# Conversion of the feed-forward weights spread over more steps of an attention and feed-forward kernel

## The chip, the cores and the metric

The kernel runs on one core of a Trainium2 chip. The metric is the device time of one execution in microseconds (us). PE is the matrix engine (TensorE), DVE is VectorE, ACT is ScalarE, POOL is GpSimd and SP is the engine that issues the DMAs (SyncE).

## The reference

Talking-heads attention over 4 batches, 12 heads, 448 positions and 64 columns a head is followed by a gated feed-forward over 1792 tokens of width 768, with a hidden width of 2048.

```python
scores = scale * np.matmul(q, k.transpose(0, 1, 3, 2))
scores = np.einsum('bhij,hg->bgij', scores, w_pre)
scores = scores - np.max(scores, axis=-1, keepdims=True)
attn = np.exp(scores)
attn = attn / (np.sum(attn, axis=-1, keepdims=True) + 1e-09)
attn = np.einsum('bhij,hg->bgij', attn, w_post)
attn_out = np.matmul(attn, v)
...
h = x @ w_in
g = h * (1.0 / (1.0 + np.exp(-1.702 * h)))
return (g @ w_out).astype(np.float32)
```

The two feed-forward weights arrive as 64-bit floats, everything else as 32-bit floats.

## The kernel before

**Steps.** The attention is cut into steps of ten query positions with all twelve heads, 120 rows a step (`GI` times `H`). A batch has 45 steps (`GPB`), the kernel 180 (`N`), and the main loop counts them in `i`. A step multiplies its gathered scores `r` by the mixing matrix on PE (`mix`, L279), takes the row maximum on DVE (`peak`, L286), the exponential on ACT (`expo`, L293), a sum correction on POOL (L299) and the reciprocal on DVE (`inverse`, L304); then it weighs the mixing matrix or the rows on POOL (L309, or L329 and L343 from the second batch on), multiplies again on PE (`post_whole` L319 in the first batch, `post` L356 to L358 after it) and copies the result (`keep_whole` L375; `keep_upper` L379 and `keep_lower` L383). Since L286 runs once a step, its rows mark the steps in the trace: the first, at 34.75 us, is step 0. The scores themselves (`scores`, L233 in 32-bit floats for batches 0 and 1, L243 in pairs of 16-bit floats for the others) are computed ahead, sent to DRAM (`sd`, L258) and gathered from there four steps ahead (`gather`, L269). `context` (L397, L408) multiplies by v. Batch 0's context is complete around step 57, so from step 58 on the loop has feed-forward work of a finished batch beside the attention of the next one.

**Feed-forward.** A unit is one slice of 256 hidden columns (`NS` = 8 slices) for one batch: 32 units, in batch order. Its work is cut into twelve quanta: six parts of the first product (`h`, L588, gate on ACT L606 and DVE L609 and L616) and six of the second (`po`, L627, collected on DVE L657 or on ACT and POOL). The loop owes 2.15 quanta a step (`RATE`) from step 58 on. What remains after step 180 runs with nothing beside it.

**Conversion of the weights.** Each slice of each kind (w_in is kind 0, w_out kind 1) has to be turned from 64-bit floats into a pair of 16-bit floats once: 16 conversions, numbered n = 2s + kind. `convert` splits one into three parts of 128x512. For each part it loads the words (L477), runs five integer or float operations on DVE (L484, L488, L492, L498, L504, tile `w_f`) and a sum of squares on ACT (L96). When the three sums are there, a small matmul joins them (L108), DVE reads the sum (L109) and derives the scale in six small operations; then ACT writes the three upper halves (`w_upper`, L532), DVE the three lower ones (`w_lower`, L537, from `w_f` too), and SP stores the pair to DRAM (L543, tile `wd`). `fetch_w` (L576) loads a slice from there for each unit (tile `wt`), one unit ahead.

**What sets the order.** Engines run their queues in order, and the order is made when the kernel is built. Conversions are jobs. In each step `run_jobs(i)` emits, after `peak` and `expo` of the step and before its `inverse`, all jobs whose first step has come, whose predecessors ran, and whose engine has tokens left (a budget of 4.3 us a step, 5.2 once feed-forward runs, at most 4.5 saved). `begin`, the argument `first` of `convert`, is the step at which the loads of a conversion may start; its two-step lag puts the DVE work two steps later. Only in those places does it act: a slice that is converted later is also fetched later, since `fetch_ahead` waits for its store.

Of the kernel before, what the change touches and what calls it, by code (L numbers as in the profile page):

```python
# [28 lines left out]
NPAIR = H // 2  # L29
NR, CP = 4, S // 4  # L30
NCC = DM // 128
NS = 8
# [6 lines left out]
def attention_then_feed_forward(ctx, tc, q, k, v, w_pre, w_post, w_in, w_out, out):  # L39
# [422 lines left out]
    EARLY = -20  # L462
# [297 lines left out]
    conv_done = {}  # L760
    for s in range(NS):
        for kind in range(2):
            n = s * 2 + kind
            conv_done[kind, s] = convert(kind, s, n * 5 - NPAIR if n > 1 else EARLY + 10 * n)


    quanta = []
# [303 lines left out]
```

## Time and profile before

| | |
|---|---|
| runs of the kernel before | 1024.65, 1029.36, 1032.99 us, median 1029.36 us |
| profiled execution | 1027.42 us, its span 1025.7 us |
| mean granted PE clock in it | 0.961 of full speed |
| busy in the span | PE 90%, DVE 61%, ACT 59%, POOL 35% |

The span lies between the first and the last instruction that the profile holds; the 1.7 us beside it are start and end. Busy shares over the span mix three stages: the first batch without feed-forward work (to 257.92 us, the start of step 58), attention and feed-forward side by side (to step 180), and feed-forward alone.

### The profile page before, as it was taken

The numbers are of one execution on the slowest core, as the hardware profiler recorded it, in microseconds if no ns is written. First come the engines' busy times: TensorE is split into PE (matmuls) and PEld (weight loads), VectorE is DVE, ScalarE is ACT, GpSimd is POOL, SyncE is SP. The second block draws the span as 40 slices with busy tenths as digits, with TensorE's granted clock in tenths as the row PEclk, the third lists the DMA queues.
The fourth block names the chain that finished last, engine by engine and source line by source line (L and its number), as shares of the span: only waits on it lengthen the run. The fifth ranks groups of instructions, "written<-read, shape, count | busy, mean of one in ns | idle before, by whom it ended". The sixth has DMA issues, their size and how long they took to land.

```text
span 1025.7 us, 19868 instructions
## 1 busy us (share of the span) xinstructions
PE 925.0 (90%) x7344; PEld 542.4 (53%) x7344; DVE 628.8 (61%) x1389; ACT 605.2 (59%) x1380; POOL 354.5 (35%) x536
## 2 busy tenths in 40 slices
PE   5678878877899889999899999999899999999998
PEld 4345555544455444555455555656455666555554
DVE  5658786698976796554644575555645565443334
ACT  3666768677577676765657657656656564323332
POOL 0111111145433455343533454334534444001221
PEclk9888999888999998999999999999999999999999
DMA  8988979768557656654676647546654341234322
GB/s 301 289 275 313 332 267 323 259 197 245 190 198 244 232 187 181 192 172 131 202 225 207 202 150 234 166 130 179 212 164 146 108 148 64 93 123 151 118 93 85
DMA packets 66565, 198.19 MB, mean 193 GB/s; under 512 B 7668, under 2 KB 32372, under 8 KB 66468
## 3 DMA queue, kind: packets, MB, share of 16 engines
q1 hardware_dynamic: 66064, 196.83, 59.4%
q8 instruction: 58, 0.95, 0.4%
q14 instruction: 39, 0.32, 0.1%
q10 hardware_dynamic: 404, 0.09, 0.1%
HBM read 140.27 MB, written 56.62 MB: 192 GB/s over the span
## 4 chain that ended last, share of the span: by engine, by line
PE 62%; DVE 17%; ACT 8%; DMA 8%; issue 3%; POOL 1%; SPq 0%; ACTq 0%; DVEq 0%; POOLq 0%
PE po L627 19%; PE h L588 18%; PE mx L279 8%; PE av L408 4%; PE qk L243 3%; PE pp L356 2%; PE pp L358 2%; PE pp L357 2%; DVE w_p L537 2%; DMA sd<-sc 2%; ACT waste L96 2%; DVE w_f L504 2%; DMA w<-in_moe_w_out_dram 2%; DVE nm L286 2%; ACT e L293 1%
## 5 line engine op out<-in xcount | busy, mean ns | idle before, releaser
L627 PE MATMUL po<-g,wt 128*128 128x448 f16 x1152 | 243.8, 355 | 11.3 <-DVE th L609 6.8
L588 PE MATMUL h<-x,wt 128*128 128x448 f16 x1152 | 244.1, 356 | 3.9 <-ACT sc L253 2.9
L279 PE MATMUL mx<-r,wa 120*120 120x448 f32 x360 | 183.3, 592 | 40.0 <-ACT e L293 29.7
L343 POOL TENSOR_TENSOR a<-w,a 120x448 f16<-120x448 f32 x135 | 150.8, 1117 | 130.2 <-issue 71.5
L627 PEld LDWEIGHTS <-wt 128*128 128x128 f16 x1152 | 109.4, 99 | 130.0 <-issue 45.1
L588 PEld LDWEIGHTS <-wt 128*128 128x128 f16 x1152 | 109.2, 98 | 117.0 <-issue 31.2
L329 POOL TENSOR_SCALAR w<-e,rs 120x448 f32<-120x448 f32 x135 | 88.2, 653 | 227.3 <-DVE rs L304 217.8
L337 ACT ACTIVATE a<-e,rs 120x448 f16<-120x448 f32 x135 | 91.0, 674 | 106.1 <-DVE rs L304 106.1
L657 DVE SCALAR_TENSOR_TENSOR acc<-po,ct,acc 128x448 f32<-128x448 f32 x141 | 96.1, 682 | 74.3 <-PE po L627 72.2
L293 ACT ACTIVATE e<-mx,nm 120x448 f32<-120x448 f32 x180 | 113.6, 631 | 31.2 <-POOL wr L309 25.4
L609 DVE SCALAR_TENSOR_TENSOR th<-th,h 128x448 f32<-128x448 f32 x64 | 39.7, 620 | 137.8 <-ACT th L606 137.8
L606 ACT ACTIVATE th<-h,ct 128x448 f32<-128x448 f32 x64 | 40.5, 633 | 140.2 <-PE h L588 129.6
L253 ACT COPY sc<-qk 120x448 f32<-120x448 f32 (+1 forms) x186 | 89.6, 532 | 41.8 <-PE qk L233 28.9
L286 DVE TENSOR_REDUCE nm<-mx 120x1 f32<-120x448 f32 x180 | 108.9, 605 | 1.9 <-PE mx L279 1.9
L356 PE MATMUL pp<-wp,a 120*112 120x120 f16 x540 | 95.7, 220 | 14.8 <-DVE p L383 14.3
L279 PEld LDWEIGHTS mx<-r,wa 120*120 120x120 f32 x360 | 61.6, 193 | 83.9 <-ACT e L293 47.0
L299 POOL TENSOR_SCALAR rs<-sm 120x1 f32<-120x1 f32 x180 | 56.8, 315 | 115.8 <-ACT e L293 103.8
L358 PE MATMUL pp<-wp,a 120*112 120x120 f16 x540 | 95.1, 219 | 0.0
L357 PE MATMUL pp<-wp,a 120*112 120x120 f16 x540 | 94.9, 218 | 0.0
L383 DVE TENSOR_TENSOR p<-pp,p 112x480 f16<-112x480 f32 x135 | 87.2, 647 | 5.9 <-ACT p L379 5.9
L356 PEld LDWEIGHTS <-a 120*112 120x112 f16 x540 | 71.5, 132 | 26.9 <-DVE p L383 12.1
L357 PEld LDWEIGHTS <-a 120*112 120x112 f16 x540 | 71.8, 133 | 15.9 <-issue 9.5
(126 smaller groups left out, 1258.1 us busy)
## 6 DMA issues: line engine op xcount, KB each, us to landing
wt<-wd SPq DMA_DIRECT2D x64, 768.0 KB
r<-sd SPq DMA_DIRECT2D x176, 210.0 KB
sd<-sc SPq DMA_DIRECT2D x72, 420.0 KB
w<-in_moe_w_in_dram SPq DMA_DIRECT2D x24, 512.0 KB
w<-in_moe_w_out_dram SPq DMA_DIRECT2D x24, 512.0 KB
wd<-w_p SPq DMA_DIRECT2D x16, 768.0 KB
sd<-sc SPq DMA_DIRECT2D x24, 308.0 KB
out_dram<-acc SPq DMA_DIRECT2D x24, 224.0 KB
```

Source lines behind the costliest of these rows:

```text
L253: (nc.scalar.copy if engs[x] == "A" else nc.vector.tensor_copy)(t[:n, x, :], two[x][:n, :S])
L279: nc.tensor.matmul(mx[:K, :S], st["wa", b][:K, :K], row.pop(("r", i))[:K, :], start=True, stop=True)
L286: nc.vector.tensor_reduce(nm[:K], row["mx", i][:K, :S], axis=AX.X, op=ALU.max, negate=True)
L293: nc.scalar.activation(e[:K], row.pop(("mx", i))[:K, :S], AF.Exp, bias=row.pop(("nm", i))[:K, 0:1], scale=1.0, accum_out=sm[:K, 0:1],)
L337: nc.scalar.activation(a1[:K], row.pop(("e", i))[:K], AF.Copy, scale=row.pop(("rs", i))[:K, 0:1])
L343: nc.gpsimd.tensor_tensor(a2[:K], row.pop(("w", i))[:K], row["a1", i][:K], op=ALU.subtract)
L356: nc.tensor.matmul(o, a1[:K, js], wp1[:K, :, :n], start=True, stop=False)
L357: nc.tensor.matmul(o, a1[:K, js], wp2[:K, :, :n], start=False, stop=False)
L358: nc.tensor.matmul(o, a2[:K, js], wp1[:K, :, :n], start=False, stop=True)
L588: nc.tensor.matmul(h, w[:, i, c, fc * 128:(fc + 1) * 128], x[:, j, c, :], start=(n == 0), stop=(n == len(terms) - 1),)
L627: nc.tensor.matmul(po, w[:, j, fc, e * 128:(e + 1) * 128], g[:, i, fc, :], start=(n == 0), stop=(n == len(terms) - 1),)
L657: nc.vector.scalar_tensor_tensor(a, po, c, a, op0=ALU.mult, op1=ALU.add)
```

## The change

One line gives each conversion its first step. Conversions 0 and 1 keep theirs. Before, conversion n began at step 5n - 6: at 4, 9, 14 and so on to 69. Now it begins at 7n - 12 up to n = 8 (2, 9, 16, 23, 30, 37, 44), and then every five and a half steps (49, 55, 60, 66, 71, 77, 82). Steps 49 on hold the loads of conversion 11 before and of conversion 9 now. Sizes, operations, and the order of the feed-forward quanta stay as they were.

```diff
     for s in range(NS):
         for kind in range(2):
             n = s * 2 + kind
-            conv_done[kind, s] = convert(kind, s, n * 5 - NPAIR if n > 1 else EARLY + 10 * n)
+            begin = EARLY + 10 * n if n < 2 else 7 * n - 12 if n <= NS else 11 * (n - NS) // 2 + 7 * NS - 12
+            conv_done[kind, s] = convert(kind, s, begin)
```

Counting the six conversion instructions on DVE (L484 to L504 and L537) by step in the two built programs gives: steps 9 to 43, 126 before and 90 now; steps 44 to 57, 46 and 44; steps 58 to 77, 57 and 59; steps 78 to 94, 8 and 44; none later. A whole conversion has 18 of them.

DVE in step 17, from one row maximum to the next, before: `w_1_p` is the pair of slice 1, `w_2_f` the words of slice 2.

```order
L286 TENSOR_REDUCE nm_921<-mx_867 120x1
L537 SCALAR_TENSOR_TENSOR w_1_p<-w_1_f_713,w_1_s,w_1_p 128x512
L537 SCALAR_TENSOR_TENSOR w_1_p<-w_1_f_719,w_1_s,w_1_p 128x512
L537 SCALAR_TENSOR_TENSOR w_1_p<-w_1_f_781,w_1_s,w_1_p 128x512
L498 SCALAR_TENSOR_TENSOR w_2_f_894<-w_2_64_1_821,w_2_f_894 128x512
L504 SCALAR_TENSOR_TENSOR w_2_f_894<-w_2_64_1_821,w_2_f_894 128x512
L304 RECIPROCAL rs_926<-rs_926 120x1
L286 TENSOR_REDUCE nm_963<-mx_911 120x1
```

The same step now.

```order
L286 TENSOR_REDUCE nm_911<-mx_860 120x1
L537 SCALAR_TENSOR_TENSOR w_1_p<-w_1_f_717,w_1_s,w_1_p 128x512
L537 SCALAR_TENSOR_TENSOR w_1_p<-w_1_f_723,w_1_s,w_1_p 128x512
L537 SCALAR_TENSOR_TENSOR w_1_p<-w_1_f_760,w_1_s,w_1_p 128x512
L304 RECIPROCAL rs_916<-rs_916 120x1
L286 TENSOR_REDUCE nm_949<-mx_901 120x1
```

The lower halves of one slice no longer share a step with the words of the next slice: the two conversions overlapped before, and now one follows the other.

DVE in step 83, before: `ct` is a unit's scale, `th` the gate, `acc` the collected output, `p` the lower half of the attention rows.

```order
L286 TENSOR_REDUCE nm_4748<-mx_4668 120x1
L600 TENSOR_SCALAR ct_4791<-ex,ew 128x1
L609 SCALAR_TENSOR_TENSOR th_0_4793<-th_0_4793,h_0_4726 128x448
L637 TENSOR_TENSOR ct_4359<-eo,ew 128x1
L657 SCALAR_TENSOR_TENSOR acc_2974<-po_0_4799,ct_4359,acc_2974 128x448
L383 TENSOR_TENSOR p_2_3900<-pp_4702,p_2_3900 112x48x10
L304 RECIPROCAL rs_4753<-rs_4753 120x1
```

The same step now.

```order
L286 TENSOR_REDUCE nm_4681<-mx_4591 120x1
L484 TENSOR_SCALAR w_7_f_4689<-w_7_64_2_4304 128x512
L488 TENSOR_SCALAR w_7_f_4689<-w_7_f_4689 128x512
L492 TENSOR_SCALAR w_7_f_4689<-w_7_f_4689 128x512
L498 SCALAR_TENSOR_TENSOR w_7_f_4689<-w_7_64_2_4304,w_7_f_4689 128x512
L504 SCALAR_TENSOR_TENSOR w_7_f_4689<-w_7_64_2_4304,w_7_f_4689 128x512
L600 TENSOR_SCALAR ct_4732<-ex,ew 128x1
L609 SCALAR_TENSOR_TENSOR th_0_4734<-th_0_4734,h_0_4659 128x448
L637 TENSOR_TENSOR ct_4267<-eo,ew 128x1
L383 TENSOR_TENSOR p_2_3801<-pp_4635,p_2_3801 112x48x10
L304 RECIPROCAL rs_4686<-rs_4686 120x1
```

Five instructions of the last w_in slice now stand ahead of the gate, of `p`'s lower half and of the reciprocal; one collection of `acc` went to ACT and POOL.

SP around the fetch of that slice for unit 7, before: `wt_7` is that slice; its store `wd_7_113` lies 21 rows above the fetch.

```order
L269 DMA r_4974<-sd_0_98 120x448
L576 DMA wt_7_4976<-wd_7_113 128x3072
L258 DMA sd_1_99<-sc_1_0_4969 120x896
L269 DMA r_5049<-sd_0_98 120x448
L269 DMA r_5137<-sd_0_98 120x448
L576 DMA wt_6_5139<-wd_6_120 128x3072
```

The same place now.

```order
L576 DMA wt_6_5111<-wd_6_120 128x3072
L258 DMA sd_1_99<-sc_1_1_5094 120x896
L269 DMA r_5202<-sd_0_98 120x448
L543 DMA wd_7_113<-w_7_p 128x3072
L269 DMA r_5295<-sd_0_98 120x448
L576 DMA wt_7_5297<-wd_7_113 128x3072
```

The store now stands one gather ahead of the fetch that reads what it wrote (steps 89 and 90; the fetch stood in step 86 before). PE's first product of unit 7 stands in step 93 in both.

## Rows read from the trace of the kernel before

**Rows 1.** The page: busy times of the engines, and two of them in 40 slices.

```profile
PE 925.0 (90%) x7344; PEld 542.4 (53%) x7344; DVE 628.8 (61%) x1389; ACT 605.2 (59%) x1380; POOL 354.5 (35%) x536
...
PE   5678878877899889999899999999899999999998
...
DVE  5658786698976796554644575555645565443334
```

**Rows 2.** Windows between steps: busy PE, PEld, DVE, ACT, POOL (instructions), PEclk, DMA share, GB/s.

```profile
63.93:192.84 128.91, 104.82 (x682) 67.11 (x681) 99.35 (x254) 92.93 (x236) 23.42 (x70) 0.92 0.88 298
...
257.92:497.81 239.89, 217.94 (x1883) 125.86 (x1883) 165.55 (x351) 163.45 (x373) 105.77 (x143) 0.96 0.62 197
389.95:463.62 73.67, 72.13 (x606) 41.94 (x604) 40.52 (x96) 48.41 (x110) 30.84 (x47) 0.98 0.64 197
497.81:721.62 223.81, 214.20 (x1936) 126.65 (x1935) 126.98 (x275) 143.49 (x330) 98.34 (x140) 0.99 0.61 187
...
300.70:384.73 84.03, 72.65 (x608) 41.37 (x606) 66.71 (x140) 59.22 (x136) 37.62 (x47) 0.98 0.70 233
538.23:609.50 71.27, 67.09 (x610) 39.80 (x608) 39.84 (x93) 49.76 (x116) 31.63 (x45) 1.00 0.61 191
```

**Rows 3.** Windows, instructions on `w_f` on DVE alone: DVE busy (instructions), PEclk, DMA, GB/s.

```profile
63.93:192.84 128.91, 68.81 (x126) 0.92 0.88 298
...
257.92:497.81 239.89, 46.58 (x65) 0.96 0.62 197
300.70:384.73 84.03, 27.38 (x37) 0.98 0.70 233
389.95:463.62 73.67, 2.94 (x3) 0.98 0.64 197
```

**Rows 4.** DVE's timeline: starts of steps 10, 12, 16 to 21, 88 and 93, one L537.

```profile
65.74 0.60 DVE L286 TENSOR_REDUCE nm<-mx 120x1 f32<-120x448 f32 x1
...
79.17 0.60 DVE L286 TENSOR_REDUCE nm<-mx 120x1 f32<-120x448 f32 x1
...
91.25 0.60 DVE L286 TENSOR_REDUCE nm<-mx 120x1 f32<-120x448 f32 x1
...
95.81 0.61 DVE L286 TENSOR_REDUCE nm<-mx 120x1 f32<-120x448 f32 x1
...
96.33 2.07 DVE L537 SCALAR_TENSOR_TENSOR w_p<-w_f,w_s,w_p 128x512 f16<-128x512 f32 x3
...
99.72 0.61 DVE L286 TENSOR_REDUCE nm<-mx 120x1 f32<-120x448 f32 x1
...
103.03 0.60 DVE L286 TENSOR_REDUCE nm<-mx 120x1 f32<-120x448 f32 x1
...
104.84 0.61 DVE L286 TENSOR_REDUCE nm<-mx 120x1 f32<-120x448 f32 x1
...
108.25 0.61 DVE L286 TENSOR_REDUCE nm<-mx 120x1 f32<-120x448 f32 x1
...
434.49 0.61 DVE L286 TENSOR_REDUCE nm<-mx 120x1 f32<-120x448 f32 x1
...
458.07 0.60 DVE L286 TENSOR_REDUCE nm<-mx 120x1 f32<-120x448 f32 x1
```

**Rows 5.** One window of eight steps, columns as in rows 2.

```profile
88.03:111.67 23.64, 22.31 (x186) 15.15 (x186) 18.95 (x51) 18.46 (x46) 4.58 (x15) 1.00 0.92 319
```

**Rows 6.** Waits from 63.93 to 192.84 us: total, times, longest.

```profile
DVE w_n L109 <- PE pp L108: 14.0, 7, 4.7
```

**Rows 7.** The page's groups by line: POOL's costliest, and the row maximum.

```profile
L343 POOL TENSOR_TENSOR a<-w,a 120x448 f16<-120x448 f32 x135 | 150.8, 1117 | 130.2 <-issue 71.5
...
L286 DVE TENSOR_REDUCE nm<-mx 120x1 f32<-120x448 f32 x180 | 108.9, 605 | 1.9 <-PE mx L279 1.9
```

**Rows 8.** SP's timeline: the fetch of `wt_7`.

```profile
422.93 0.35 SPq L576 DMA_DIRECT2D wt<-wd  x1
```

**Rows 9.** The chain that ended last, from 30 to 430 us: its longest store.

```profile
49.80 9.79 DMA wd<-w_p
```

## The prediction

> **What bounds the kernel now.** I read the page first, then windows cut at the starts of steps, then DVE's timeline inside them. The page shows PE busy 90% of the span, but its slices show PE at 5 to 8 tenths and DVE at 5 to 9 in the first ten, and the reverse from the twentieth on [rows 1]. So a mean says little here: the change takes work out of one stage and puts it into another, and each has its own limit.
>
> L286 runs once a step, 180 times [rows 7], so step numbers can be turned into times. Two stretches matter, because the count of instructions in the order says so: 36 conversion instructions on DVE, two conversions of 18, leave steps 9 to 43 and come back in steps 78 to 94. Elsewhere the counts change by two instructions, up in one stretch and down in another.
>
> Steps 9 to 43 take 128.91 us; PE is busy 104.82 of it, DVE 99.35, ACT 92.93, and the DMA engines have a share of 0.88 [rows 2]. No engine is full; they take turns. A step without conversion work lasts 1.81 us (from 63.93, where that window begins, to 65.74), while the five steps from 91.25 to 108.25 last 4.56, 3.91, 3.31, 1.81 and 3.41, together 17.00, with one conversion among them [rows 4]. In the long ones DVE is the last to end: the reciprocal and the next row maximum stand behind the words of a slice in its queue, and exponential, POOL and the next matmul wait for them. But PE has no room either: in the eight steps from 88.03 to 111.67 it is busy 22.31 of 23.64 us [rows 5].
>
> In steps 80 to 94 PE is busy 72.13 of 73.67 us, DVE only 40.52 [rows 2]. PE is the bound there, and three conversion instructions are left in it [rows 3].
>
> **The change, first stretch.** Price of what leaves: 68.81 us over 126 instructions is 546 ns each [rows 3], so 36 of them are 19.7 us of DVE time. Two joins go with them, at which DVE waited for PE's small matmul 14.0 us in seven times, 2.0 each [rows 6]. The six sums and six upper halves on ACT, the six loads and two stores on SP's queue go too; with a DMA share of 0.88 that cannot hurt here.
>
> How much of it is on the path has two bounds. Upper: step lengths alone. The new cycle has seven steps: eight words of a slice in one (4.56 as step 16), six instructions in the next (6 x 0.546 and a row maximum of 0.60, 3.88), one instruction that fits into the gap (1.81), an empty step (1.81), the join (3.41), the upper halves on ACT (1.81), and the three lower halves (2.07 and 0.60, 2.67) [rows 4, 7]; the sum is 19.95. Five such cycles in place of seven of 17.00 give 99.8 for 119.0: a gain of 19.2 us. Lower: PE's idle time alone. It is 128.91 - 104.82 = 24.1 us. Steps 10 and 11 take 13.43 together [rows 4], 7.4 more than PE's mean of 2.99 a step; the first loads are late there, and the change does not thin them out. The other 16.7 us over 126 instructions are 0.132 each, 4.8 us for 36. I take **9 us**, nearer to the lower end, because the light steps that the change makes cannot last 1.81 us where a step carries scores and context: PE's own mean is 2.99, and the window of eight steps shows it almost full [rows 2, 5].
>
> **The change, second stretch.** The same 36 instructions cost more here: 46.58 us over 65 is 717 ns each against 546 [rows 3], so 25.8 us of DVE. What runs beside them differs: in steps 9 to 43 POOL is busy 18% of the time, in steps 80 to 94 it is 42% [rows 2]. The Trainium skill (SBUF — State Buffer, Who interferes with whom) says that DVE and POOL share a pair of ports as an exclusive lock, and that the second to come is blocked until the first is done; an estimate by it, half of POOL's 1117 ns operation [rows 7] in 42% of the cases, would make 546 into 781 ns, and the 25.8 us into 28.1. The trace agrees in direction and gives the smaller number, so the sum stays with the row.
>
> How much of 25.8 us is on the path: lower bound nothing, since DVE idles 73.67 - 40.52 = 33.2 us in steps 80 to 94 [rows 2]; upper bound all of it. Between them two comparisons of like with like. Steps 58 to 102 and 103 to 147 are two batches with the same attention and feed-forward work; the first has 65 conversion instructions more and takes 239.89 instead of 223.81 us [rows 2, 3]: 16.1 / 65 = 0.247 each. Steps 65 to 78 and 110 to 123, where the next batch's q and k are also converted, take 84.03 and 71.27 with 37 instructions more [rows 2, 3]: 0.345 each. For 36 that is 8.9 and 12.4 us. Steps 78 to 94 have little of the q and k work, so I take the longer comparison, **9 us**. The mechanism: a burst of five to eight instructions holds up `keep_lower`, the gate and the collection of outputs behind it in DVE's queue, PE finds its result banks taken, and waits. In step 83 of the new order five words stand ahead of all three.
>
> The rest is small. Steps 44 to 57 lose two instructions and steps 58 to 77 gain two, under 1 us by the prices above. Four collections of outputs move from DVE to ACT and POOL in steps 58 to 102, off the path as far as ACT has room (163.45 of 239.89 busy) [rows 2]. From step 95 on the order is the same.
>
> **Sum.** 9 us less and 9 us more: **no change**. The profiled execution was 1027.42 us, its span 1025.7, and the median of the runs 1029.36; the forecast lies between the two, 1028.
>
> **Rival 1, faster: the second stretch hides everything.** DVE has 33.2 us idle where 25.8 arrive. If the bursts fall into gaps in which PE works through its quanta, the cost is about 1 us and the gain of the first stretch stays: 9 to 19, at 13 in the middle a time of 1016. For it: DVE is 55% busy there and ACT 66% [rows 2]. Against it: conversions in steps 58 to 78 also met idle DVE time (66.71 of 84.03 busy in steps 65 to 78) and still cost 0.345 each. The Trainium skill (Perfetto Trace Analysis, Optimization Strategy) holds that interleaving stretches with different bounds may improve a kernel; here that would be this rival in full, and the traces before bear out only part of it. Chance 0.17.
>
> **Rival 2, slower: DVE's bursts stop a full PE.** PE has 1.5 us to spare in steps 80 to 94 against 11 in steps 65 to 78 [rows 2], so a delay there finds no slack on PE. If 21 of the 25.8 us reached the path and 9 came back from the first stretch, the time would be 1040. It decides from 19 us on, three quarters of the DVE time, where the loss passes 1%; the rows show 35 to 48%. Chance 0.10, which also holds the case that the first stretch gives back only its lower bound and the second costs 15.
>
> **Rival 3, still within 1%: the last w_in slice comes late.** Its fetch for unit 7 was issued at 422.93 us, in step 86, for a product in step 93, which begins at 458.07 [rows 4, 8]. Now its lower halves stand in step 88, which begins at 434.49 [rows 4], its store in step 89, its fetch in step 90, and the fetch waits for the store. The longest store in the chain took 9.79 us [rows 9]. Counted on the old times, and allowing 6 us from the start of step 88 to the end of the lower halves, 10 for the store and 10 for a fetch of the same size, the slice is there at about 460: PE would stand 2 us, and 10 us if both transfers met the gathers. I give it 0.08 inside the forecast's own share; it would add 2 to 8 us. w_out's last slice is later too, but is not needed before step 103.
>
> **How the numbers follow.** Forecast with its own spread (gain 5 to 14, cost 5 to 13) 0.73, from 1019 to 1036; rival 1 0.17, rival 2 0.10. About 1% (10 us) is what a measurement of this kernel can tell from no change; the three runs shown lie 8.3 us apart. Faster by over 1% is rival 1, slower is rival 2. The range takes in the middle of rival 1 and stops short of rival 2: 1015 to 1038.
>
> **What would show each step.** The window of steps 9 to 43 should last 115 to 124 us, with PE busy some 105 and DVE about 78; the conversion instructions there still near 546 ns. Steps 80 to 94 should last about 8 us longer than 73.67, with PE's busy time unchanged, DVE near 66 and the conversion instructions near 717 ns. Steps 58 to 77 and everything behind step 103 should be as before. A first stretch near 110 us would show that PE's idle time was the wrong bound; a second stretch of 75 us that idle DVE time was free after all; a PE wait in front of unit 7's first product that rival 3 happened. The forecast is wrong altogether if PE's granted clock changes: 0.92 in steps 9 to 43 and 0.98 in steps 80 to 94 [rows 2] leave some 8 us in the first, if denser work brought it to full speed.

## The result and the profile after

| | before | after |
|---|---|---|
| median of 15 runs | 1029.36 us | 1037.54 us |
| all runs | 1024.49 to 1033.23 us | 1029.87 to 1042.00 us |
| profiled execution, its span | 1027.42, 1025.7 us | 1036.89, 1035.2 us |
| forecast | | 1028, 1015 to 1038 us |

The ratio is 1.0082, 95% interval 1.0058 to 1.0106. The changed kernel is slower by some 8 us: inside 1% and inside the range, but not the forecast "no change". The spans differ by 9.5 us.

Page of the changed kernel, answering to [rows 1]: PE, and PE and DVE in 40 slices.

```profile
PE 931.4 (90%) x7344; PEld 546.1 (53%) x7344; DVE 636.0 (61%) x1387; ACT 606.7 (59%) x1382; POOL 359.0 (35%) x540
...
PE   6688897877988888899899999999899999999998
...
DVE  5667665598867798765654566555755555443334
```

The same 7344 matmuls keep PE busy 6.4 us longer (925.0 before), at a lower mean clock (0.955 against 0.961); idle time rises by the other 3.1. Next come windows cut at the same steps as [rows 2], columns as there: steps 9 to 43, 44 to 57, 58 to 79, 80 to 94, 65 to 78, 103 to 147.

```profile
66.53:192.70 126.17, 104.26 (x677) 66.99 (x675) 79.05 (x207) 84.88 (x215) 20.89 (x70) 0.92 0.81 267
192.70:251.73 59.03, 45.72 (x358) 28.31 (x359) 48.74 (x106) 41.57 (x97) 28.27 (x41) 0.88 0.72 233
251.73:388.82 137.09, 120.23 (x938) 68.00 (x938) 111.21 (x217) 92.04 (x210) 58.43 (x72) 0.91 0.63 209
388.82:473.97 85.15, 73.99 (x633) 42.87 (x632) 64.70 (x142) 58.18 (x132) 38.27 (x51) 0.96 0.63 195
295.42:383.60 88.18, 77.44 (x608) 43.82 (x605) 67.52 (x141) 58.95 (x135) 37.49 (x47) 0.90 0.68 230
507.26:731.08 223.82, 214.21 (x1936) 126.52 (x1935) 126.96 (x275) 143.27 (x330) 98.59 (x140) 0.99 0.60 185
```

Two stretches of the kernel before that the prediction had held to be level, steps 44 to 57 and 58 to 79:

```profile
192.84:257.92 65.08, 49.82 (x360) 30.52 (x361) 50.80 (x116) 42.22 (x99) 27.70 (x41) 0.82 0.71 220
257.92:389.95 132.03, 114.22 (x934) 64.57 (x934) 107.00 (x214) 92.75 (x212) 59.33 (x72) 0.95 0.62 205
```

Length of each stretch, from row maximum to row maximum, with the difference split into PE's busy and idle time:

| steps | before | after | difference | busy | idle |
|---|---|---|---|---|---|
| to the end of 8 | 63.93 | 66.53 | +2.60 | | |
| 9 to 43 | 128.91 | 126.17 | -2.74 | -0.56 | -2.18 |
| 44 to 57 | 65.08 | 59.03 | -6.05 | -4.10 | -1.95 |
| 58 to 79 | 132.03 | 137.09 | +5.06 | +6.01 | -0.95 |
| 80 to 94 | 73.67 | 85.15 | +11.48 | +1.86 | +9.62 |
| 95 to 102 | 34.19 | 33.29 | -0.90 | | |
| 103 on | | | 0 | | |

Of the first line 2.06 us are scatter: step 0, ahead of which the change moves nothing, begins at 36.81 us in place of 34.75, and anywhere from 34.4 to 36.2 in the other profiles below. The other 0.54 lie in steps 0 to 8, where the words of conversion 2 now stand in steps 4 to 6 and no longer in 6 to 8; the prediction left these steps out. For the rest, 8.8 us come back before step 58 and 15.6 go behind it. The forecast had 9 and 9.

Other runs below keep one of the two orders up to step 57, so they show how far a row of the table repeats. Steps 9 to 43 take 129.50 and 129.18 us in e2 and e4 (order of before), 127.07, 127.29 and 129.08 in e1, e5 and e6 (changed order): the gain there is 1.8 us on average. Steps 44 to 57 take 65.16 and 65.06 against 58.64, 57.03 and 59.01: that gain repeats.

DVE's conversion instructions alone, as [rows 3], in steps 9 to 43, 44 to 57, 80 to 94 and 65 to 78: 49.31 over 90 is 548 ns, and 28.55 over 39 is 732 ns.

```profile
66.53:192.70 126.17, 49.31 (x90) 0.92 0.81 267
192.70:251.73 59.03, 30.93 (x44) 0.88 0.72 233
388.82:473.97 85.15, 28.55 (x39) 0.96 0.63 195
295.42:383.60 88.18, 27.43 (x37) 0.90 0.68 230
```

DVE's waits in steps 9 to 43, with [rows 6] for the kernel before (total, times, longest):

```profile
DVE rs L304 <- POOL rs L299: 21.8, 18, 3.5
DVE w_n L109 <- PE pp L108: 11.3, 5, 4.6
DVE w_f L484 <- DMA w<-in_moe_w_out_dram: 7.7, 2, 4.1
...
DVE w_f L484 <- DMA w<-in_moe_w_in_dram: 0.5, 1, 0.5
```

The last two lines are the surprise: DVE stands 8.2 us for words that have not landed (2.6 before). The two long ones in DVE's timeline, in steps 11 and 39:

```profile
76.34 0.43 DVE L484 TENSOR_SCALAR w_f<-w 128x512 int32<-128x512 int32 x1 [3.62 <-DMA w<-in_moe_w_out_dram]
...
173.56 0.43 DVE L484 TENSOR_SCALAR w_f<-w 128x512 int32<-128x512 int32 x1 [4.08 <-DMA w<-in_moe_w_out_dram]
```

Their loads were issued at 69.64 and 164.41 us, 6.7 and 9.2 us earlier. In steps 80 to 94 PE's longest waits, of 11.2 us idle, are these (before: 0.7 and 0.6 us):

```profile
PE qk L243 <- DVE th L609: 3.9, 1, 3.9
PE pp L356 <- DVE p L383: 3.1, 3, 1.2
PE po L627 <- ACT pt L651: 1.8, 1, 1.8
```

The longest falls into step 81. Six words of a slice stand ahead of the gate L609 in DVE's queue there, and PE's scores L243 wait for the bank that this gate reads:

```profile
394.68 0.83 DVE L504 SCALAR_TENSOR_TENSOR w_f<-w,w_f 128x512 int32<-128x512 int32 x1
395.44 1.25 DVE L484 TENSOR_SCALAR w_f<-w 128x512 int32<-128x512 int32 x1
...
398.99 0.61 DVE L609 SCALAR_TENSOR_TENSOR th<-th,h 128x448 f32<-128x448 f32 x1
```

```profile
399.65 0.90 PE L243 MATMUL qk<-kp,qp 64*120 64x448 f16 x3 [3.94 <-DVE th L609]
```

In step 84, seven words stand ahead of gate, collection and `p`'s lower half, and the step lasts 8.51 us (4.50 before).

### The profile page after: what moved, and what is told of

Its sections match the earlier page's. It is cut to its first block, busy times and chain, and to the rows that moved or that the text cites. A ratio compares the mean times of both kernels' runs of the same rounds, so it can differ in the third digit from the quotient of the medians.

```text
span 1035.2 us, 19869 instructions
## 1 busy us (share of the span) xinstructions
PE 931.4 (90%) x7344; PEld 546.1 (53%) x7344; DVE 636.0 (61%) x1387; ACT 606.7 (59%) x1382; POOL 359.0 (35%) x540
## 4 chain that ended last, share of the span: by engine, by line
PE 62%; DVE 20%; ACT 7%; DMA 6%; issue 3%; POOL 1%; ACTq 0%; SPq 0%; DVEq 0%; POOLq 0%
PE po L627 19%; PE h L588 17%; PE mx L279 9%; PE av L408 4%; PE qk L233 3%; PE qk L243 2%; PE pp L356 2%; DVE w_f L498 2%; DMA w<-in_moe_w_out_dram 2%; PE pp L358 2%; PE pp L357 2%; DVE nm L286 2%; DVE w_f L484 2%; PE pp L319 2%; DVE p L383 2%
## 5 line engine op out<-in xcount | busy, mean ns | idle before, releaser
L627 PE MATMUL po<-g,wt 128*128 128x448 f16 x1152 | 247.7, 359 | 13.6 <-DVE th L609 6.2
L279 PE MATMUL mx<-r,wa 120*120 120x448 f32 x360 | 183.5, 593 | 34.1 <-ACT e L293 21.8
L657 DVE SCALAR_TENSOR_TENSOR acc<-po,ct,acc 128x448 f32<-128x448 f32 x137 | 93.3, 681 | 71.9 <-PE po L627 69.9
L609 DVE SCALAR_TENSOR_TENSOR th<-th,h 128x448 f32<-128x448 f32 x64 | 39.6, 619 | 129.9 <-ACT th L606 129.9
L253 ACT COPY sc<-qk 120x448 f32<-120x448 f32 (+1 forms) x186 | 89.8, 533 | 49.9 <-PE qk L233 30.1
L356 PE MATMUL pp<-wp,a 120*112 120x120 f16 x540 | 96.7, 221 | 20.1 <-DVE p L383 19.6
L279 PEld LDWEIGHTS mx<-r,wa 120*120 120x120 f32 x360 | 61.2, 191 | 76.0 <-ACT e L293 34.2
L299 POOL TENSOR_SCALAR rs<-sm 120x1 f32<-120x1 f32 x180 | 54.5, 303 | 129.6 <-ACT e L293 117.7
L358 PE MATMUL pp<-wp,a 120*112 120x120 f16 x540 | 96.0, 220 | 0.0
L357 PE MATMUL pp<-wp,a 120*112 120x120 f16 x540 | 95.9, 220 | 0.0
L357 PEld LDWEIGHTS <-a 120*112 120x112 f16 x540 | 72.4, 134 | 16.7 <-issue 10.5
```

The source lines that it names most:

```text
L279: nc.tensor.matmul(mx[:K, :S], st["wa", b][:K, :K], row.pop(("r", i))[:K, :], start=True, stop=True)
L356: nc.tensor.matmul(o, a1[:K, js], wp1[:K, :, :n], start=True, stop=False)
L357: nc.tensor.matmul(o, a1[:K, js], wp2[:K, :, :n], start=False, stop=False)
L358: nc.tensor.matmul(o, a2[:K, js], wp1[:K, :, :n], start=False, stop=True)
L627: nc.tensor.matmul(po, w[:, j, fc, e * 128:(e + 1) * 128], g[:, i, fc, :], start=(n == 0), stop=(n == len(terms) - 1),)
L657: nc.vector.scalar_tensor_tensor(a, po, c, a, op0=ALU.mult, op1=ALU.add)
```

## The experiments

Theories named in the expectations: **L**, the words of a slice come later than DVE wants them; its rival **P**, steps 9 to 43 are set by PE and its clock. For the stretches behind step 58: the **sum** of conversion work on DVE counts, or the **bursts** of it in one step, or its **position** within the step. A ratio is to the kernel before, measured beside each.

**e1 and e2: how dear are the moved conversions?** Both leave out the conversion of the last slice, after and before, and use slice 6's weights in its place.

```diff
-    for s in range(NS):
+    for s in range(NS - 1):
         for kind in range(2):
...
-        nc.sync.dma_start(out=wt[kind, u], in_=wd[kind, units[u][0]])
+        nc.sync.dma_start(out=wt[kind, u], in_=wd[kind, min(units[u][0], NS - 2)])
```

> The changed kernel without its last two conversions (both kinds of slice 7; slice 7 is computed with slice 6's converted weights, so the products keep their number and shape). This leaves the change's first stretch alone. In the two profiles steps 9 to 43 went from 128.9 to 126.2 us, steps 44 to 57 from 65.1 to 59.0, steps 80 to 94 from 73.7 to 85.2. Theory A, the first stretch gives back little and the second costs what the two conversions' 26 us of DVE time cost on a full PE: 3 to 8 us below the kernel before, 12 to 15 below the changed one, steps 80 to 94 back at 74 us. Theory B, the first stretch gives back the 9 us of the prediction or more and the loss comes from somewhere else (granted clock, luck of the profiled run): 9 to 15 us below the kernel before, and steps 80 to 94 above 78 us.

Measured: 1023.56 us, ratio 0.9930 (0.9908 to 0.9951), 14.0 us under the changed kernel. Steps 80 to 94 of e1:

```profile
389.86:460.80 70.94, 69.45 (x603) 40.64 (x601) 40.42 (x97) 48.35 (x110) 30.80 (x47) 1.00 0.66 205
```

Without the 36 instructions the stretch is full again (69.45 of 70.94) and 14.2 us shorter. That is Theory A, with the stretch 3 us below the 74 that it expected.

> The kernel before without its last two conversions (same replacement of slice 7's weights). It prices two conversions where they stood before, steps 66 to 82. Theory A, a conversion costs the same anywhere beside the feed-forward (0.25 to 0.35 us for each of 36 instructions): 9 to 12 us below the kernel before. Theory C, steps 66 to 82 have room that steps 80 to 94 lack, so the move was from cheap or equal places to a dear one: 3 to 6 us below the kernel before.

Measured: 1016.22 us, ratio 0.9870 (0.9838 to 0.9903). Steps 58 to 79 fall from 132.03 to 122.00 and 80 to 94 from 73.67 to 68.77: 14.9 us for 36 instructions there too, 0.41 us each and not the 0.247 of the forecast. The medians of e2 and of the kernel before beside it (1031.16) differ by 14.9 us as well: more than the 9 to 12 of Theory A, and far from Theory C. The two runs hold the same 14 conversions at the two sets of places, and differ by 7.3 us. So the loss is not the last slice's alone: in steps 58 to 79, e1 holds 64 conversion instructions and takes 138.58 us, e2 holds 29 and takes 122.00.

**e3: words fetched two steps earlier in the changed kernel.**

```diff
-            begin = first + a if first == EARLY else first
-            before = [(job(begin, None, 0, lambda a=a: fetch(a), stage=("w64", users)), 2)]
+            begin = first + a if first == EARLY else first - 2 if first > 4 else first
+            before = [(job(begin, None, 0, lambda a=a: fetch(a), stage=("w64", users)), 4 if first > 4 else 2)]
```

> The changed kernel with each slice's words loaded two steps earlier (lag of four steps in place of two; the DVE work stands in the same steps up to step 61). In the changed kernel DVE waits 8.2 us for words in steps 9 to 43, and exponentials and reciprocals behind it. Theory L, late words are what ate the first stretch's gain: 5 to 8 us faster than the changed kernel, those waits gone. Theory P, the light steps are bound by PE and by the chain row maximum, exponential, sum, reciprocal in any case: 0 to 2 us faster, the time turns up as waits for POOL's sums and PE.

Measured: 1020.70 us, ratio 0.9907 (0.9883 to 0.9931), 16.8 us under the changed kernel. Window and longest waits of DVE in steps 9 to 43:

```profile
64.15:181.24 117.09, 100.36 (x677) 65.11 (x675) 79.04 (x207) 84.57 (x215) 21.00 (x70) 0.96 0.85 284
```

```profile
DVE rs L304 <- POOL rs L299: 23.7, 20, 3.5
DVE w_n L109 <- PE pp L108: 9.9, 5, 4.5
```

The waits for words are gone, and the stretch loses 9.1 us: 5.2 of PE's idle time and 3.9 of its busy time, as the granted clock rises from 0.92 to 0.96. The whole gained more than the 5 to 8 us of Theory L; in the two profiles 2.4 of it lie ahead of step 9, mostly scatter, and 2.8 in steps 58 to 79, where the edit shifts instructions too.

**e9: the other way, words one step later.**

```diff
-            begin = first + a if first == EARLY else first
-            before = [(job(begin, None, 0, lambda a=a: fetch(a), stage=("w64", users)), 2)]
+            begin = first + a if first == EARLY else first + 1 if 4 < first <= 44 else first
+            before = [(job(begin, None, 0, lambda a=a: fetch(a), stage=("w64", users)), 1 if 4 < first <= 44 else 2)]
```

> The changed kernel with the words of the conversions before step 45 fetched one step later than now (the lag between a slice's load and its first instruction is one step in place of two). Theory L (the first stretch lost its gain because the words come after their step has begun): steps 9 to 43 take 131 to 136 us in place of 126, DVE's waits for the words grow from 8 us to 15 or more, and the whole comes to 1042 to 1047 us. Theory P (the stretch is set by PE's work and the clock, the waits are covered): within 2 us of the changed kernel, 1036 to 1040 us.

Measured: 1046.40 us, ratio 1.0171 (1.0151 to 1.0190). Steps 9 to 43 take 135.06 us, with these waits of DVE:

```profile
DVE w_f L484 <- DMA w<-in_moe_w_out_dram: 12.4, 3, 6.3
...
DVE w_f L484 <- DMA w<-in_moe_w_in_dram: 4.4, 2, 2.6
```

With no wait for words the stretch takes 117.09, with 8.2 us of it 126.17, with 16.8 us 135.06: every microsecond of this wait costs about 1.07. Other runs lie on the same line: e7 and e12, also without the wait, take 117.94 and 116.89, and e1, e5 and e6, with 8.5 to 9.1 us of it, 127.07 to 129.08. Theory L holds, and P falls.

**e4: at most three conversion instructions a step from step 58, in the kernel before.** Words and lower halves are marked as parts (lines left out here), and a step takes no more than three of them. The later runs use the same edit with other numbers.

```diff
+        words = 0
...
+                if j.get("part") and x_done and words >= 3:
+                    continue
...
+                words += "part" in j
```

> The kernel before with at most three conversion instructions on DVE in any step once feed-forward work runs (five to eight before); the same work, so it ends at step 88 in place of 82. Theory burst, a burst ahead of the lower half, the gate and the collection in DVE's queue is what stops PE: 4 to 8 us faster than the kernel before, fewer PE waits on p's lower half. Theory sum, each instruction's time counts however it is spread: within 2 us, steps 80 to 94 longer by what steps 58 to 79 get shorter.

Measured: 1023.27 us, ratio 0.9922 (0.9900 to 0.9944). Steps 58 to 79 fall from 132.03 to 126.60; steps 80 to 94 stay (73.46), though 16 conversion instructions now stand there in place of 3. Against the kernel before beside it (1031.16) that is 7.9 us, as theory burst expected; PE's waits for `p`'s lower half in steps 58 to 79 fall only from 9.9 to 7.8 us.

**e5: in the changed kernel from step 58, the conversion's instructions at the end of their step,** behind `p`'s lower half and the reciprocal. The loads of the words are put off with them (first line).

```diff
+            before[0][0]["part"] = True
...
+                if j.get("part") and x_done and i >= FROM:
+                    put_off.append(j["f"])
...
+        for f in put_off:
+            f()
+        put_off.clear()
```

> The changed kernel with the conversion instructions of a step, once feed-forward runs (from step 58 on), issued at the end of the step, behind p's lower half and the reciprocal, in place of ahead of them; same steps, same bursts. The kernel without the two moved conversions left 80 to 94 at 70.9 us against 85.2, so they cost 14 us there, more than half of their DVE time. Theory position: what hurts is that they stand ahead of the lower half, the gate and the collection. Then steps 80 to 94 fall to 74 to 78 us and steps 58 to 79 by 3 or more, 10 us or more faster than the changed kernel. Theory sum: DVE's next row maximum waits for them instead, steps 80 to 94 stay at 82 to 87, within 3 us of the changed kernel.

Measured: 1058.39 us, ratio 1.0264 (1.0234 to 1.0293); steps 58 to 79 take 151.13 and 80 to 94 95.16 us. Position as a remedy falls, and the result is outside theory sum too, which expected no more than 3 us: what stands last in a step stands ahead of the next step's row maximum, which exponential, POOL and PE wait for. ACT's longest wait in steps 58 to 94 shows it; the changed kernel has no such wait there:

```profile
ACT e L293 <- DVE nm L286: 36.0, 13, 4.4
```

The loads were moved too, and SP stands 27.1 us for words' buffers (20.1 in the changed kernel); how much of the loss that is was not tried.

**e6: at most four a step from step 58, in the changed kernel.**

> The changed kernel with at most four conversion instructions on DVE in a step once feed-forward runs (five to eight before), ahead of the lower half as they were. Theory burst, PE has slack for about 2.5 us of extra DVE work a step and none for 4 to 5: steps 80 to 94 at 76 to 80 us, steps 58 to 79 at 130 to 133 in place of 137, together 8 to 12 us faster than the changed kernel. Theory sum: within 3 us, the time returns in the steps that get the rest.

Measured: 1027.90 us, ratio 0.9978 (0.9960 to 0.9996). Windows of steps 58 to 79 and 80 to 94:

```profile
252.80:379.38 126.58, 112.66 (x937) 64.19 (x937) 112.13 (x219) 88.58 (x204) 57.63 (x71) 0.97 0.68 221
379.38:462.59 83.21, 71.17 (x601) 41.82 (x600) 66.00 (x143) 57.10 (x132) 36.25 (x50) 0.98 0.64 202
```

In the first, 10.5 us are gone: 7.6 of PE's busy time (clock 0.91 to 0.97) and 2.9 of its idle time. In the second only 1.9, and PE still idles 12.0: the 76 to 80 us that theory burst expected there were missed, the 130 to 133 before it were beaten, and the whole is 9.6 us under the changed kernel. So bursts decide in steps 58 to 79; in steps 80 to 94 a limit of four gains little.

**e7 and e8: early words and at most four a step,** from step 58 (e7) or throughout (e8).

> The changed kernel with words loaded two steps earlier (it gave 1020.7 us) and at most four conversion instructions a step once feed-forward runs. If the two causes are separate (late words in the first stretch, bursts in the second), their gains add: 1010 to 1014 us. If early words gained in the second stretch, or bursts hurt only because of late words, 1017 to 1021.

> The same, with at most four conversion instructions in every step, the first batch's too. There a step of eight lasts 4.56 us and a light one is bound by PE's 2.9 us or by the 1.8 us chain. Theory PE bound: four instructions (2.2 us and a row maximum of 0.6) hide behind PE's share of a step, so steps 9 to 43 fall from 117 to 106 to 111 us, 6 to 10 us faster than the run before it. Theory chain: each step with words grows by what DVE does, 4 x 0.55 against a gap of 1.1 us, and nothing is won: 115 to 119 us.

Measured: e7 1023.10 us, ratio 0.9930 (0.9906 to 0.9954); e8 1023.39 us, ratio 0.9934 (0.9917 to 0.9952). e7 misses both of its ranges. The gains are there in their places (e8: 113.26 us in steps 9 to 43, the shortest of all, between its two theories), but e8 as a whole gains nothing on e7: it takes 132.78 us in steps 58 to 79 (e7 127.88). And in both the last w_out slice now ends so late that steps 95 to 109 take 82.71 (e7) and 82.12 us (e8) in place of 73.72. SP's queue, ACT and PE there, in e7:

```profile
SPq L578 <- DMA wd<-w_p: 7.5, 1, 7.5
```

```profile
487.12 1.43 SPq L120 DMA_DIRECT2D vb<-in_v_dram  x3
```

```profile
ACT vp L193 <- DMA vb<-in_v_dram: 6.3, 2, 4.6
```

```profile
PE po L629 <- ACT sc L253: 6.4, 1, 6.4
```

The fetch stands 7.5 us for the slice's store and is issued at 485.85 us. The loads of the next `v` (`vb`) stand behind it in SP's queue; ACT waits 6.3 us for them, its copy of the scores (L253) comes late, and PE waits for the bank that this copy empties. So PE stands, but not for the slice itself, as rival 3 had it.

**e12: as e7, but a slice of one kind every four and a half steps after the first batch,** so that the last one ends earlier.

```diff
-            begin = EARLY + 10 * n if n < 2 else 7 * n - 12 if n <= NS else 11 * (n - NS) // 2 + 7 * NS - 12
+            begin = EARLY + 10 * n if n < 2 else 7 * n - 12 if n <= NS else 9 * (n - NS) // 2 + 44
```

> The changed kernel with its seven steps between slices through the first batch, words fetched two steps earlier, then a slice of one kind every four and a half steps, at most four conversion instructions in a step from step 58. If what the run with early words and four instructions a step lacked was its late last slice: 1009 to 1013 us and steps 95 to 110 back at 72 to 75 us. If the two gains exclude one another for another reason: 1019 us or more, with steps 95 to 110 at 72 to 75 us all the same.

Measured: 1028.07 us, ratio 0.9991 (0.9967 to 1.0016): a miss. Steps 95 to 109 are back at 73.72, so the late slice is what had made them long. But steps 44 to 57 and 80 to 94, into which the conversions were pulled ahead, take more (59.47 and 83.71 in e7):

```profile
184.03:248.21 64.18, 48.86 (x358) 29.08 (x359) 52.60 (x113) 42.28 (x100) 29.71 (x42) 0.81 0.77 237
380.34:468.50 88.16, 77.31 (x636) 44.50 (x635) 65.09 (x143) 56.73 (x130) 36.19 (x49) 0.94 0.60 189
```

**e11: early words, at most four a step, six steps between slices in the first batch and five after it** (`6 * n - 9` up to n = 8, then `5 * (n - NS) + 39`).

> The changed kernel with words fetched two steps earlier, a slice of one kind every six steps through the first batch and every five after it, and at most four conversion instructions in a step. If the gains of early words and of few instructions in a step add where no slice ends late: 1005 to 1012 us, with no wait of PE for the last slice in steps 95 to 110. If the number of instructions in the steps from 80 on decides alone: 1018 to 1024 us.

Measured: 1015.56 us, ratio 0.9861 (0.9841 to 0.9880), between its two expectations, 3.6 us above the range of adding gains. Steps 80 to 94 hold 30 conversion instructions and take 76.87 us, only 3.2 more than before; steps 95 to 109 show no late slice (72.16).

**e10: the kernel before, its places kept, with at most four a step before step 58 and three from there.**

> The kernel before, with its places for the slices, but at most four instructions of a conversion in a step before step 58 and at most three from there. If what pays is how few instructions stand in one step, and not where a slice begins: steps 9 to 43 take about 115 us in place of 129, steps 58 to 79 about 126 in place of 132, and the whole comes to 1008 to 1014 us. If the distance between the slices is what pays: steps 9 to 43 stay at 127 to 129 and the whole at 1020 to 1024 us.

Measured: 1012.50 us, ratio 0.9840 (0.9824 to 0.9856): the fastest of all, 25 us under the changed kernel. Its windows of steps 9 to 43, 44 to 57, 58 to 79 and 80 to 94:

```profile
61.50:182.78 121.28, 100.42 (x678) 64.72 (x676) 96.46 (x250) 90.11 (x230) 23.87 (x70) 0.97 0.91 305
182.78:240.42 57.64, 43.65 (x352) 26.31 (x352) 50.20 (x111) 42.26 (x100) 27.14 (x41) 0.91 0.80 254
240.42:371.08 130.66, 117.99 (x949) 66.59 (x950) 105.01 (x212) 88.39 (x203) 60.19 (x72) 0.95 0.65 210
371.08:448.06 76.98, 70.45 (x599) 41.04 (x596) 52.60 (x116) 51.93 (x119) 30.87 (x46) 0.98 0.63 196
```

The total fell as expected, the parts only in sign: 121.28 where 115 was expected, 130.66 where 126 was; steps 44 to 57 gave 7.4 that nobody had counted, and steps 80 to 94, which now hold 18 conversion instructions in place of 3, lost 3.3. The conversion work is what it was, and so are the first steps of the slices; what paid is that fewer instructions stand in one step. By it, DVE's waits in steps 9 to 43 fall as well: for words from 2.6 to 1.3 us, for the joins from 14.0 to 9.7.

## Why the prediction was wrong

The step that failed is the price of the second stretch: 0.247 us for each instruction, 9 us for 36, and under 1 us for steps 58 to 77. Behind step 58 the change cost 15.6 us, and two conversions left out there gave 14.2 (e1) and 14.9 us (e2). The 9 us of the first stretch failed too (2.74), but a gain elsewhere made up for it.

**First stretch, "9 us, bounds 4.8 to 19.2": 2.74.** The price per instruction held (548 ns for 546), and PE and DVE were busy what was forecast (104 and 79 us). The window was to last 115 to 124 us and lasted 126.17. The term was mis-sized by a wait that the sum did not hold: the words of two slices came 6.7 and 9.2 us after their loads, and the two steps ahead of them (9 and 10, 37 and 38) now last 5.6 and 6.1. The prediction noted late loads in steps 10 and 11 and took them as unchanged; they grew from 2.6 to 8.2 us. Without the wait (e3) the gain is 11.8 us, inside the bounds. e3 and e9 show this from both sides. Why these two loads took longer than others was not tried; in SP's queue the second stands right behind three loads of `v`, issued at 161.98 us. One reading of the prediction is off as well: its window "of eight steps" [rows 5] holds 14 matmuls of L279, two a step, and so seven steps.

**Second stretch, "9 us, bounds 0 to 25.8": 11.48 in steps 80 to 94, and the step before the number failed.** The comparison behind 0.247 us each held that steps 58 to 102 and 103 to 147 have "the same attention and feed-forward work". They have not. PE's groups of the kernel before in the two stretches (line, engine, shape, count, busy us, mean ns):

```profile
L588 PE MATMUL h<-x,wt 128*128 128x448 f16 x283 | 63.5, 365 | 3.9 <-ACT sc L253 2.9 <-ACT pt L651 1.0
L627 PE MATMUL po<-g,wt 128*128 128x448 f16 x252 | 55.7, 358 | 2.3 <-DVE th L609 1.3 <-ACT pt L651 0.8
```

```profile
L627 PE MATMUL po<-g,wt 128*128 128x448 f16 x288 | 63.1, 357 | 6.6 <-ACT sc L253 3.5 <-DVE th L609 3.1
L588 PE MATMUL h<-x,wt 128*128 128x448 f16 x289 | 61.8, 352 | 0.0
```

The first has 535 feed-forward matmuls and the second 577: 42 less, at 0.357 us 15.0 us of PE work. Its scores take 3.8 us more (22.4 against 18.6, 36 of them in 32-bit floats). So a PE that had 11.2 us less to do still took 16.1 longer: (16.1 + 11.2) / 65 is 0.42 each, and 36 cost 15.1 us. e2 measured 14.9, and e1 14.2. That something differed was in the counts of [rows 2], 1883 matmuls against 1936. The correction alone does not prove the price: it takes PE to be the bound throughout, and the prediction's shorter comparison, corrected in the same way, goes down. Steps 65 to 78 have 190 feed-forward matmuls against 186 in steps 110 to 123 (1.4 us) and 2.1 us more of scores, so (12.8 - 3.5) / 37 is 0.25 in place of 0.345. The price rests on e1 and e2.

**Steps 44 to 57, "under 1 us": -6.05; steps 58 to 77, "under 1 us": +5.06 to step 79.** Counting instructions missed both, since the number hardly changed and their places did. In the kernel before, five conversion instructions stand in step 43 ahead of `x` (L431), for which PE's context waits 4.64 us; PE is busy 0.38 of the step's 4.95 us and then works at half clock. Steps 43 to 45 before, and after:

```profile
187.89:192.84 4.95, 0.38 (x4) 0.19 (x2) 4.71 (x16) 3.64 (x11) 0.56 (x2) 0.94 0.94 307
192.84:196.59 3.75, 3.68 (x20) 2.52 (x21) 0.76 (x4) 1.33 (x4) 0.92 (x3) 0.50 0.97 337
196.59:203.67 7.08, 7.08 (x57) 5.14 (x57) 1.68 (x10) 2.30 (x6) 0.19 (x1) 0.83 0.68 225
```

```profile
187.35:192.70 5.35, 3.60 (x32) 2.28 (x30) 2.96 (x18) 3.59 (x9) 0.56 (x2) 1.00 0.75 224
192.70:195.72 3.02, 2.86 (x20) 1.87 (x21) 0.77 (x4) 2.32 (x5) 0.92 (x3) 0.68 0.88 294
195.72:200.71 4.99, 4.99 (x38) 3.56 (x37) 2.69 (x6) 2.29 (x6) 0.19 (x1) 0.85 0.62 204
```

In step 44 the same 20 matmuls take 3.68 us at a clock of 0.50 (1.2 GHz) and 2.86 at 0.68. Of the 6.05 us, 4.10 are PE's busy time. e10 keeps the places of before, spreads the burst, and has 57.64 us there. In steps 58 to 79 it goes the other way: the idle time hardly changed, and 6.01 us are matmuls at 0.91 instead of 0.95; e6 takes the bursts away and gets them back. The last paragraph of the prediction named the clock as what would make it wrong, but looked for it in steps 9 to 43, where it stayed at 0.92, and 80 to 94, where it fell from 0.98 to 0.96; steps 44 to 79, where it counted most, it passed over.

**Sum.** Up to step 57 the forecast gain of 9 came as 8.8, by accident: 2.7 where it was expected and 6.05 where none was. Behind step 58 the cost was 15.6 and not 9.

**Rival 1** (hidden) did not happen: of 25.6 us of added DVE time 11.5 were paid. The Trainium skill (Perfetto Trace Analysis, Optimization Strategy) says that interleaving stretches with different bounds may improve a kernel. No run here bears that out: the plain move loses 0.8%, and with thinned bursts e10, which leaves the slices' places alone, is faster (1012.50 us) than e11, which moves work behind step 43 (1015.56). **Rival 2** has its mechanism and not its size: PE in steps 80 to 94 idles 11.2 us in place of 1.5, behind words that stand ahead of gate and collection (step 81); with 11.5 to 14.2 us it stays short of its 19. **Rival 3** did not happen in the changed kernel, because everything moved: the fetch was issued at 447.55 us and the first product in step 93 began at 469.42, with a wait of 0.42 for something else. In e7 and e8 a late slice did cost PE time, by the way of SP's queue that is shown there.

**What stays open.** Steps 58 to 102 with the same 103 conversion instructions take 255.53 (after), 252.04 (e3), 248.76 (e7) and 244.32 us (e6); with 107 in e8 252.26, with 97 in e12 253.58, with 89 in e11 242.79. What differs between them, besides the time of the loads, is the steps into which the instructions fall; no run gives a rule for steps 80 to 94. Of the 16.9 us by which e12 exceeds e11 in steps 44 to 94, 8.8 are PE's busy time (240.88 against 232.11 us); why its clock fell to 0.81 in steps 44 to 57 was not tried.

## What to carry to other kernels

Count what one step holds, not only what a stretch holds: with the places left alone and the bursts of eight cut to four and three, this kernel gains 1.6%, and moving the same bursts apart lost 0.8%. When the distance between steps changes, turn every lag that is counted in steps back into microseconds and compare it with the time that the load takes. Before two stretches are compared "like with like", compare their counts of the bounding engine's instructions by line.

## What was not expected of the hardware

A wait can come back as slower matmuls: the first 8.2 us of waiting for words cost 9.1, of which 3.9 were PE's busy time (clock 0.92 against 0.96). It need not: the next 8.6 (e9) cost 8.9, of which 1.3 were busy time, at 0.91. Executions of one kernel scatter along with the mean clock: the 15 of the changed kernel run from 1029.87 us at 0.963 to 1042.00 at 0.952, though not in strict order.

The conversion instructions stay dearer where POOL works: 548 ns where it is busy 17% of the time, 732 ns where 45%. The trace of the changed kernel shows how. In step 81, L484 takes 1.25 us (0.42 in most steps), and it begins while this operation of POOL runs:

```profile
395.14 1.27 POOL L343 TENSOR_TENSOR a<-w,a 120x448 f16<-120x448 f32 x1 [0.16 <-POOL w L329]
```

Over the whole trace, L488 takes 0.42 to 0.43 us in all 41 cases with no POOL operation of about 1 us beside it, and 1.04 on average in the five that begin while one runs. The Trainium skill (SBUF — State Buffer, Who interferes with whom) states that the port pair which DVE shares with GpSimd is an exclusive lock, and that who comes second is blocked until the first is done. The trace agrees.
